# One column's rank-one term by the matmul engine in eight rounds, and a passage between two experts written in another order

## The chip, the core and the metric

The kernel runs on one core of one Trainium2 chip. Five engines work beside each other, each on a queue of its own: TensorE (PE, matmuls; its weight loads are listed as PEld), VectorE (DVE), ScalarE (ACT), GpSimd (POOL) and SyncE (SP), which sends the DMAs here. They wait for one another by semaphores. The metric is the device time of one execution in microseconds (us), the median over several runs.

## The reference

The kernel must compute this (numpy):

```
X = real(fft(fft(x, axis=1), axis=2))        # x: 2 x 3008 x 256
x = X.reshape(6016, 256)
h = x @ moe_w_in                              # 256 -> 2048
y = (h / (1 + exp(-h))) @ moe_w_out           # 2048 -> 256
h = y @ moe2_w_in                             # 256 -> 2048
g = max(h, 0) + moe2_alpha * min(h, 0)
out = g @ moe2_w_out                          # 2048 -> 256
```

Everything is fp32 outside the matmuls. To keep the accuracy of fp32, a factor of a matmul is split in two parts of type fp32r: `hi`, a rounded copy, and `lo`, the source less `hi`. A product is then three matmuls: hi by hi, lo by hi, hi by lo.

## The kernel before, in words

**Stages.** The transform is done as matrix products (64 by 47 points along the sequence, then 256 columns), with the symmetry of a real transform: tokens stand in pairs, and the 256 features are folded into sums and differences, 128 rows each. Of the 256 features, column 128 is left over by the folding. The 6016 tokens are six chunks of 502 pairs. A chunk's transformed features come out of PE as `ce` (even part), `co` (odd part) and `cn` (column 128, the same number on every row). ACT copies the first two into the hi parts of a tile `eo` (line 167, in `split`), DVE makes the low parts, and ACT copies `cn` into `n` (line 380).

**Expert 1** is 96 rounds, one for each chunk and each of 16 blocks of 128 hidden columns; `ORDER` lists them. The first eight rounds are blocks 0 to 7 of chunk 0. A round i does:
- `eo_mm`: the products `pe` (three matmuls, lines 562 to 564) and `po` (three) in PSUM;
- `silu_split`: DVE adds column 128's term, `t = n * w128 + pe` (line 570), where w128 is a column of 128 weights; then hp = t + po and t = t - po (lines 573, 574), the hidden values of the two tokens of a pair; ACT makes SiLU of each twice, as `gh` rounded and as fp32 (lines 577, 578);
- `low1` for the round before: the low parts `gl` of its two tiles (line 590), on POOL or DVE by `lo_pool`;
- `mm2` for the round two back (`LAG`): twelve matmuls with the weights `wo` into four accumulators (lines 612 to 616).

**Other work among the rounds.** The weights arrive as 64-bit numbers in pairs of 32-bit words (`raw_i`, `raw_o`, `w_raw`), and five steps turn a piece into fp32: ACT line 183, then four on DVE, the third on line 199. The pieces' splits, the transform of the other chunks (`z` is its middle stage, line 345 on ACT and 347 on DVE), and the preparation of expert 2's weights are divided among the rounds by `PLAN`: `put(a, b, steps)` spreads steps over rounds a to b - 1.

**Expert 2** goes by another scheme, in 96 items: seven products of sums and differences of blocks in place of eight, on `os` tiles (split sums of the first expert's output, made by `split_o1`, lines 650 to 660) and slabs `ws_*` of prepared weights (lines 514 to 523). Its items follow in written order: `outer` (two products into `ac`, which ACT copies to `e`, line 690), `inner` (three products), `seventh`, `fourth`, the PReLU by ACT and DVE, and `mm4`. Its output weights `wo` come from `v2o` by two sign steps on ACT for each half slab (line 542, scale by a column of `fc`) and a split (line 167 on ACT, 168 on POOL). The **passage** is where the last rounds of expert 1 (`mm2` of rounds 94 and 95) stand among the first items of expert 2.

**What sets the order.** The start, up to the first chunk's `eo` and n, and all of expert 2 are in written order (`tc.manual_schedule`). The rounds are ordered by a scheduler that plays the program on a time line; `leash` holds a round's extra steps behind given instructions of the rounds before. Within an engine's queue, nothing overtakes. SP's DMAs report on eight semaphores taken in turn (DMAHW0 to DMAHW7), and a DMA waits until the last one on its semaphore has landed.

## Time and profile before

| | us |
|---|---|
| median of 3 runs (lowest to highest) | 976.97 (976.53 to 977.37) |
| the profiled execution | 975.78 |
| its span on the core | 974.0 |
| mean granted TensorE clock | 0.996 of full speed |
| PE busy | 953.6 (98%) |
| DVE busy | 785.1 (81%) |
| ACT busy | 709.3 (73%) |
| POOL busy | 424.6 (44%) |

The span is what the profiler saw on the engines; the execution's own time has 1.8 us more around it. A row of a time line gives start, duration, engine, line, operation, output tile <- inputs, the shape, and in brackets the idle time of the engine ahead of it with what ended it. Several instructions of one form that follow each other stand as one row (x2). A tile's number is left out: `gl` stands for each of them. A wait put down to an instruction is the one that came last.

### The profile page before, as it was taken

The numbers are of one execution on the slowest core, as the hardware profiler recorded it, in microseconds if no ns is written. First come the engines' busy times: TensorE is split into PE (matmuls) and PEld (weight loads), VectorE is DVE, ScalarE is ACT, GpSimd is POOL, SyncE is SP. The second block draws the span as 40 slices with busy tenths as digits, with TensorE's granted clock in tenths as the row PEclk, the third lists the DMA queues.
The fourth block names the chain that finished last, engine by engine and source line by source line (L and its number), as shares of the span: only waits on it lengthen the run. The fifth ranks groups of instructions, "written<-read, shape, count | busy, mean of one in ns | idle before, by whom it ended". The sixth has DMA issues, their size and how long they took to land.

```text
span 974.0 us, 14393 instructions
## 1 busy us (share of the span) xinstructions
PE 953.6 (98%) x5186; PEld 821.7 (84%) x5186; DVE 785.1 (81%) x1319; ACT 709.3 (73%) x1410; POOL 424.6 (44%) x368
## 2 busy tenths in 40 slices
PE   8899999999999999999899999999999999999998
PEld 6578888788788888887789999999999999999997
DVE  5977888787696988997588787887878888787876
ACT  3557677575575757778788787888888888887875
POOL 2576889753257677799522131221222112131200
PEclk9989999999999999999999999999999999999999
DMA  8822000015101110100000000000000000000000
GB/s 269 284 78 87 1 1 22 22 28 174 44 1 60 44 61 27 44 1 1 1 1 22 1 22 23 1 22 1 23 22 1 22 1 22 22 1 22 1 23 21
DMA packets 16615, 37.06 MB, mean 38 GB/s; under 512 B 1824, under 2 KB 11296, under 8 KB 14880
## 3 DMA queue, kind: packets, MB, share of 16 engines
q1 hardware_dynamic: 16544, 36.15, 11.2%
q8 instruction: 40, 0.66, 0.3%
q14 instruction: 31, 0.25, 0.1%
HBM read 26.83 MB, written 9.31 MB: 37 GB/s over the span
## 4 chain that ended last, share of the span: by engine, by line
PE 87%; DVE 3%; POOL 3%; ACT 3%; issue 2%; DMA 0%; SPq 0%; POOLq 0%; DVEq 0%; ACTq 0%
PE a L772 27%; PE ac L674 20%; PE a L614 7%; PE a L616 7%; PE a L612 7%; PE b L674 3%; PE po L562 2%; PE po L564 2%; PE pe L562 2%; PE po L563 2%; PE pe L564 2%; PE pe L563 2%; POOL gl L590 2%; PE psb L327 1%; PE psa L283 1%
## 5 line engine op out<-in xcount | busy, mean ns | idle before, releaser
L772 PE MATMUL a<-gh,wo 128*128 128x502 f32 x768 | 268.2, 391 | 0.0
L772 PEld LDWEIGHTS a<-gh,wo 128*128 128x128 f32 x768 | 145.1, 189 | 23.3
L741 DVE SCALAR_TENSOR_TENSOR h<-h,fc,q 128x502 f32<-128x502 f32 x192 | 129.9, 676 | 38.0 <-ACT q L736 35.3
L590 POOL TENSOR_TENSOR gl<-t,gh 128x502 fp32r<-128x502 f32 x96 | 133.6, 1392 | 55.4 <-ACT t L578 44.5
L614 PE MATMUL a<-gl,wo 128*128 128x502 f32 x384 | 148.6, 396 | 4.0 <-POOL gl L590 2.9
L772 PE MATMUL a<-gl,wo 128*128 128x502 f32 x384 | 149.7, 391 | 0.0
L616 PE MATMUL a<-gh,wo 128*128 128x502 f32 x384 | 146.6, 392 | 0.0
L577 ACT ACTIVATE gh<-hp 128x502 fp32r<-128x502 f32 x96 | 59.8, 623 | 116.5 <-DVE hp L573 115.5
L752 DVE TENSOR_TENSOR gl<-h,gh 128x502 fp32r<-128x502 f32 x192 | 140.7, 733 | 0.1
L612 PE MATMUL a<-gh,wo 128*128 128x502 f32 x384 | 119.2, 393 | 2.4 <-ACT gh L577 2.3
L747 ACT ACTIVATE gh<-h 128x502 fp32r<-128x502 f32 x192 | 118.4, 617 | 2.1 <-DVE h L741 2.1
L590 POOL TENSOR_TENSOR gl<-hp,gh 128x502 fp32r<-128x502 f32 x65 | 90.1, 1386 | 68.1 <-ACT hp L578 66.5
L736 ACT ACTIVATE q<-h,fc 128x502 f32<-128x502 f32 x192 | 116.9, 609 | 2.8 <-DVE h L719 1.5
L650 POOL TENSOR_TENSOR xt<-o 128x252 f32<-128x252 f32 x24 | 16.7, 715 | 187.2 <-ACT q L736 149.8
L614 PEld LDWEIGHTS a<-gl,wo 128*128 128x128 f32 x384 | 73.1, 190 | 21.6 <-POOL gl L590 5.1
L570 DVE SCALAR_TENSOR_TENSOR t<-n,sm,pe 128x502 f32<-128x502 f32 x96 | 70.3, 732 | 25.5 <-PE pe L564 23.6
L612 PEld LDWEIGHTS a<-gh,wo 128*128 128x128 f32 x384 | 71.8, 189 | 18.7 <-ACT gh L577 4.0
L616 PEld LDWEIGHTS a<-gh,wo 128*128 128x128 f32 x384 | 73.1, 190 | 14.6
L772 PEld LDWEIGHTS a<-gl,wo 128*128 128x128 f32 x384 | 72.4, 189 | 7.6
L708 ACT ACTIVATE u<-ac 128x252 f32<-128x252 f32 x96 | 36.6, 381 | 54.2 <-PE ac L674 54.2
L573 DVE TENSOR_TENSOR hp<-t,po 128x502 f32<-128x502 f32 x96 | 64.5, 672 | 13.9 <-PE po L564 6.8
L660 POOL TENSOR_TENSOR os<-o,os 128x252 fp32r<-128x252 f32 x36 | 32.4, 912 | 92.4 <-ACT os L659 92.4
(191 smaller groups left out, 2294.0 us busy)
## 6 DMA issues: line engine op xcount, KB each, us to landing
out_t<-ot SPq DMA_DIRECT2D x24, 251.0 KB, 2.6
x<-in_xs SPq DMA_DIRECT2D x8, 512.0 KB, 5.4
raw_i<-in_wi SPq DMA_DIRECT2D x8, 512.0 KB, 6.2
raw_w<-in_wi SPq DMA_DIRECT2D x4, 1024.0 KB, 5.9
raw_w<-in_wo SPq DMA_DIRECT2D x4, 1024.0 KB, 4.8
raw_o<-in_wo SPq DMA_DIRECT2D x3, 1024.0 KB, 6.8
y<-ys SPq DMA_DIRECT2D x16, 144.0 KB, 3.4
x<-in_xs SPq DMA_DIRECT2D x2, 1024.0 KB, 4.7
```

Source lines behind the costliest of these rows:

```text
L570: nc.vector.scalar_tensor_tensor(t, E128[c], w128_sb[:, f : f + 1], pe, op0=ALU.mult, op1=ALU.add)
L573: nc.vector.tensor_tensor(hp, t, po, op=ALU.add)
L590: LAST["gl", i] = (nc.gpsimd if s or lo_pool(i + 1) else nc.vector).tensor_tensor(lo, h, hi.bitcast(F32), op=ALU.subtract)
L612: nc.tensor.matmul(ACC1[lb, s], hi, G[i, s][0], start=st, stop=False)
L614: nc.tensor.matmul(ACC1[lb, s], hi, G[i, s][1], start=False, stop=False)
L616: nc.tensor.matmul(ACC1[lb, s], lo, G[i, s][0], start=False, stop=sp)
L674: nc.tensor.matmul(to, w, x, start=start and q == 0, stop=q == 2, skip_group_check=True)
L736: nc.scalar.activation(h["q", i][:, to], source(n, part), AF.Abs, scale=coef(n, i, 1))
L741: nc.vector.scalar_tensor_tensor(h[f"h{i}"][:, to], source(n, part), coef(n, i, 0), h["q", i][:, to], op0=ALU.mult, op1=ALU.add)
L747: nc.scalar.activation(hi, H[n][f"h{i}"], AF.Copy)
L752: nc.vector.tensor_tensor(lo, H[n][f"h{i}"], G[n, i][0].bitcast(F32), op=ALU.subtract)
L772: nc.tensor.matmul(ACC2[lb], w[lb][j], x, start=st and first, stop=sp and last)
```

## The change

Two things are changed that have nothing to do with each other.

**Column 128 in the first eight rounds.** A tile `rank` of 96 rows is added. Its first 1024 columns (`RANK["w"]`) hold the weights of column 128 for hidden blocks 0 to 7: the hi part on row 0, the lo part on row 32, hi again on row 64, zeros elsewhere. The next 502 (`RANK["x"]`) hold n of chunk 0: its hi part on rows 0 to 63, its low part on rows 64 to 95. One matmul of 96 rows adds hi by hi, lo by hi and hi by lo to `pe`. ACT copies `pe` into t, and DVE's step on line 570 goes for these rounds. To fill the tile, the row of weights is loaded once more as 16 x 128 (`wrow`), turned into fp32 and split (`rank_split`); six DMAs on SP bring four rows at a time, as one row, into two cleared tiles `rank_s` (`rank_place`), and ACT copies those into `rank` (`rank_round`), ahead of the first chunk's `eo`.

**The passage.** The sign steps of expert 2's output weights get steps of their own in rounds 84 to 92 (`sg0` to `sg3`), where before they went with the splits; the splits of slabs 2 and 3 go to items 98 to 101, counted on from the 96 rounds. `split_o1(0)` is spread over rounds 89 to 93 in place of 91 to 94. `gl` of the last round is made by DVE for both tiles.

```diff
@@ -29,7 +29,8 @@
     "fa": (16, 17), "x": (24, 27, 32, 34), "a": (30, 33, 36, 38), "y0": (41, 42), "c3": (43, 48), "y1": (49, 50), "c4": (54, 61),
     "y2": (65, 66), "c5": (67, 77), "w2": (50, 88),
     "co": (60, 61), "ws0": (62, 80), "ws0b": (84, 92), "ws1": (80, 92), "ws1b": (93, 99),
-    "wo0": (86, 87), "wo1": (90, 91), "wo2": (97, 98), "wo3": (98, 100),
+    "sg0": (84, 86), "sg1": (87, 89), "sg2": (89, 91), "sg3": (91, 93),
+    "wo0": (86, 88), "wo1": (90, 92), "wo2": (98, 100), "wo3": (100, 102),
 }
 W2_AHEAD = 2
 HALF = 252
...
@@ -59,6 +60,7 @@
 A_VEC = lambda b, h, i: b and h and i == 0
 W2_ORDER = (0, 2, 4, 5, 1, 3, 6, 7)
 LO_POOL = 30
+RANK_F = 8
 K_PARTS = (0, 12, 24, 32)
 B_GROUPS = (0, 3, 6, 9, 12, 16)
 PAIRS = [(k0 + i, k0 + (k1 - k0) // 2 + i) for k0, k1 in zip(K_PARTS, K_PARTS[1:]) for i in range((k1 - k0) // 2)]
...
@@ -377,7 +382,12 @@
 
         def ny():
             E128[b * NCB + c] = n = ep.tile([128, CW], F32, tag="e128", name=f"n{b}_{c}", padded_shape=[128, 512])
-            LAST[b * NCB + c] = nc.scalar.activation(n, part("n", (ch, SG0, 0), (ch, SG0, 1)), AF.Copy)
+            ps = part("n", (ch, SG0, 0), (ch, SG0, 1))
+            if b * NCB + c == 0:
+                to = RANK["x"]
+                nc.scalar.activation(to, ps[:96], AF.Copy)
+                nc.vector.tensor_tensor(to[64:96], ps[64:96], to[64:96].bitcast(F32), op=ALU.subtract)
+            nc.scalar.activation(n, ps, AF.Copy)
 
         return [mixed] * (b > 0 or c == 2) + [ev, od, ny]
 
...
@@ -531,25 +541,56 @@
         return steps
 
     def prep_wo2(g):
-        def part(h):
-            if h == 0:
-                wo_tiles(2, g)
+        def signs(h):
             o = (g % 2) * 1024 + h * 512
             v = V2["o", g // 2][:, o : o + 512]
             for q in range(2):
                 f = 4 * g + 2 * h + q
                 w = v[:, 256 * q : 256 * q + 256]
                 nc.scalar.activation(w, w, AF.Copy, scale=fc[:, 2, f : f + 1])
+
+        def part(h):
+            if h == 0:
+                wo_tiles(2, g)
+            o = (g % 2) * 1024 + h * 512
+            v = V2["o", g // 2][:, o : o + 512]
             hi, lo = (WO[2, g, j].rearrange("p f e -> p (f e)")[:, h * 512 : h * 512 + 512] for j in range(2))
             split(hi, lo, v, nc.gpsimd)
 
-        return [lambda: part(0), lambda: part(1)]
+        return [lambda: signs(0), lambda: signs(1)], [lambda: part(0), lambda: part(1)]
 
 
     ACC1 = {}
     G = {}
     O1 = {}
     MORE = [False]
+
+    def rank_rows():
+
+        t = big([96, 2048], F32R, "rank")
+        RANK["w"], RANK["x"] = t[:, : 128 * RANK_F], t[:, 1024 : 1024 + CW]
+        u = xp.tile([128, 512], F32, tag="xs", name="rank_f")
+        RANK["f"] = [u[:NF, 128 * j : 128 * j + 128] for j in range(3)]
+        RANK["s"] = [xp.tile([128, 512], F32, tag="xs", name=f"rank_s{j}") for j in range(2)]
+        for u in RANK["s"]:
+            nc.gpsimd.memset(u[:96], 0.0)
+
+    def rank_split():
+        f, hi, lo = RANK["f"]
+        nc.scalar.activation(hi.bitcast(F32R), f, AF.Copy)
+        nc.vector.tensor_tensor(lo, f, hi, op=ALU.subtract)
+
+    def rank_place():
+        for n, u in enumerate(RANK["s"]):
+            for r, j in ((0, 0), (32, 1), (64, 0)):
+                nc.sync.dma_start(
+                    u[r : r + 1, :].rearrange("p (f m) -> p f m", m=128),
+                    RANK["f"][1 + j][4 * n : 4 * n + 4],
+                )
+
+    def rank_round():
+        for n, u in enumerate(RANK["s"]):
+            nc.scalar.activation(RANK["w"][:, 512 * n : 512 * n + 512], u[:96], AF.Copy)
 
     def eo_mm(i):
         c, f = ORDER[i]
...
@@ -561,13 +602,19 @@
             hi, lo = WI[1, g, j][:, sl], WI[1, g, j + 1][:, sl]
             nc.tensor.matmul(ps, hi, eo[:, j, :], start=True, stop=False)
             nc.tensor.matmul(ps, lo, eo[:, j, :], start=False, stop=False)
-            LAST["pe", i] = nc.tensor.matmul(ps, hi, eo[:, j + 1, :], start=False, stop=True)
+            whole = j or i >= RANK_F
+            LAST["pe", i] = nc.tensor.matmul(ps, hi, eo[:, j + 1, :], start=False, stop=bool(whole))
+        if i < RANK_F:
+            LAST["pe", i] = nc.tensor.matmul(pe, RANK["w"][:, 128 * f : 128 * f + 128], RANK["x"], start=False, stop=True)
         return pe, po
 
     def silu_split(i, pe, po):
         c, f = ORDER[i]
         t = work(F32, f"t{i}")
-        nc.vector.scalar_tensor_tensor(t, E128[c], w128_sb[:, f : f + 1], pe, op0=ALU.mult, op1=ALU.add)
+        if i < RANK_F:
+            nc.scalar.activation(t, pe, AF.Copy)
+        else:
+            nc.vector.scalar_tensor_tensor(t, E128[c], w128_sb[:, f : f + 1], pe, op0=ALU.mult, op1=ALU.add)
         low1(i - 1)
         hp = work(F32, f"hp{i}")
         nc.vector.tensor_tensor(hp, t, po, op=ALU.add)
...
@@ -584,10 +631,11 @@
     def low1(i):
         if i < 0:
             return
+        end = i == len(ORDER) - 1
         for s in range(2):
             hi, h = G[i, s]
             lo = work(F32R, f"gl{i}_{s}")
-            LAST["gl", i] = (nc.gpsimd if s or lo_pool(i + 1) else nc.vector).tensor_tensor(
+            LAST["gl", i] = (nc.gpsimd if not end and (s or lo_pool(i + 1)) else nc.vector).tensor_tensor(
                 lo, h, hi.bitcast(F32), op=ALU.subtract
             )
             G[i, s] = (hi, lo)
...
@@ -819,15 +868,19 @@
             load_o1(1)
             warm(cs[:, FA0 : FA0 + 128], cs[:, :256], WARM)
             (s0, p0), (s1, p1) = prep_o1(0)
+            rank_rows()
+            wrow_st = to_f32(lambda: RANK["f"][0], ("wrow", 0, 128), "wrow")[1]
             w128_st = to_f32(lambda: w128_sb, ("w128", 0, NF), "w128")[1]
             run(i00[:4])
             run(i01[:2])
-            run(w128_st[:1])
+            run(w128_st[:1] + wrow_st[:1])
             nc.scalar.activation(ch, cc, AF.Copy)
             run(i00[4:])
             for ab in zip(i01[2:], w128_st[1:]):
                 run(ab)
-            run(w128_st[4:])
+            run(w128_st[4:] + wrow_st[1:])
+            rank_split()
+            rank_place()
             nc.vector.tensor_tensor(cl, cc[:, : SG0 - CD0], ch.bitcast(F32)[:, : SG0 - CD0], op=ALU.subtract)
             for n, (st, pool) in enumerate(zip(after_i0, SUM0)):
                 (st if callable(st) else st[pool == "v"])()
...
@@ -838,6 +891,7 @@
             run(b01[:2])
             run(p0)
             run(s1[:EARLY_O0])
+            rank_round()
             run(stage_c(0, 0))
             rest(1)
             for h in range(2):
...
@@ -908,8 +962,10 @@
             put(*PLAN[f"ws{pg}"], steps[:8])
             put(*PLAN[f"ws{pg}b"], steps[8:])
         for g in range(4):
-            put(*PLAN[f"wo{g}"], prep_wo2(g))
-        put(n1 - 5, n1 - 1, split_o1(0))
+            first, then = prep_wo2(g)
+            put(*PLAN[f"sg{g}"], first)
+            put(*PLAN[f"wo{g}"], then)
+        put(n1 - 7, n1 - 2, split_o1(0))
 
         for i in range(n1):
             pe, po = eo_mm(i)
```

What is left out: the new input `wrow` (column 128's weights as 16 x 128), its raw tile and its load behind that of `w128`.

**How the order moves.** The rows that follow are the instructions as they stand in an engine's queue: line of the code, operation, output <- inputs, partitions x elements; x2 is two in a row.

SP at the start of the program, behind the load of the second piece of expert 1's weights (`raw_o`, `raw_i`). `ys` and `y` are stores and loads that carry the first chunk between two stages of the transform. In brackets stand the semaphores that a DMA waits on (here with the compiler's number). Before:

```order
L404 DMA raw_o_190<-in_wo 128x1024
L395 DMA raw_i_198<-in_wi 128x1024 x2
L395 DMA raw_o_201<-in_wo 128x2048 [waits DMAHW0_49]
L297 DMA ys_0_1_130<-ya_0_132 48x12x128 [waits DMAHW1_49]
L297 DMA ys_1_1_137<-ya_1_139 48x12x128 [waits DMAHW2_49]
```

The same place after the change:

```order
L414 DMA raw_o_192<-in_wo 128x1024
L405 DMA raw_i_200<-in_wi 128x1024 x2
L405 DMA raw_o_203<-in_wo 128x2048 [waits DMAHW1_49]
L586 DMA rank_s_228<-rank_f 1x4x128 [waits DMAHW2_49,Activation_49,Pool_49]
L586 DMA rank_s_228<-rank_f 1x4x128 [waits DMAHW3_49,DVE_49]
L586 DMA rank_s_228<-rank_f 1x4x128 [waits DMAHW4_49]
L586 DMA rank_s_229<-rank_f 1x4x128 [waits DMAHW5_49,Pool_49]
L586 DMA rank_s_229<-rank_f 1x4x128 [waits DMAHW6_49]
L586 DMA rank_s_229<-rank_f 1x4x128 [waits DMAHW7_49]
L302 DMA ys_0_1_132<-ya_0_134 48x12x128 [waits DMAHW0_49]
```

The six DMAs into `rank_s` stand between the last load of weights and the stores of `ys`; the last of them is the eighth DMA behind the first `raw_i` of this place and goes by the same semaphore.

ACT ahead of the first chunk's `eo`; `wo` and `cvo` are expert 1's output weights, z the middle stage of the transform. Before:

```order
L345 ACTIVATE z_1_271<-psb_1_3_283 128x63
L452 ACTIVATE wo_0_0_291<-cvo_0_251 128x512
L183 ACTIVATE cvo_1_295<-raw_o_190 128x512
L167 ACTIVATE eo_0_299<-ce_0_300 128x502
L167 ACTIVATE eo_0_299<-co_0_308 128x502
L380 ACTIVATE n_0_314<-cn_0_315 128x502
```

The same place after the change:

```order
L350 ACTIVATE z_1_292<-psb_1_3_304 128x63
L462 ACTIVATE wo_0_0_312<-cvo_0_272 128x512
L186 ACTIVATE cvo_1_316<-raw_o_192 128x512
L593 ACTIVATE rank<-rank_s_228 96x512
L593 ACTIVATE rank<-rank_s_229 96x512
L170 ACTIVATE eo_0_322<-ce_0_323 128x502
L170 ACTIVATE eo_0_322<-co_0_331 128x502
L388 ACTIVATE rank<-cn_0_338 96x502
L390 ACTIVATE n_0_337<-cn_0_338 128x502
```

Both copies of `rank_s` stand ahead of the first `eo`, and the copy of n into `rank` ahead of n.

POOL in the last rounds of expert 1, from the second `gl` of round 92 on: `v2w` and `ws_*` are expert 2's input weights, `os` the low parts of its first sums. Before:

```order
L590 TENSOR_TENSOR gl_1_4330<-t_4286,gh_1_4298 128x502
L523 TENSOR_TENSOR v2w_3354<-v2w_3354 128x512
L518 TENSOR_TENSOR ws_5l<-v2w_3354,ws_5h 128x512
L660 TENSOR_TENSOR os_1_4303<-o_0_741,os_0_4302 128x252 x2
L590 TENSOR_TENSOR gl_1_4373<-t_4326,gh_1_4338 128x502
L518 TENSOR_TENSOR ws_7l<-v2w_3354,ws_7h 128x512
L660 TENSOR_TENSOR os_1_4303<-xt_0_4261,os_0_4302 128x504
L660 TENSOR_TENSOR os_1_4303<-xt_1_4262,os_0_4302 128x504
L590 TENSOR_TENSOR gl_1_4416<-t_4369,gh_1_4381 128x502
L590 TENSOR_TENSOR gl_1_4432<-t_4412,gh_1_4424 128x502
```

The same place after the change:

```order
L638 TENSOR_TENSOR gl_1_4377<-t_4332,gh_1_4344 128x502
L533 TENSOR_TENSOR v2w_3387<-v2w_3387 128x512
L528 TENSOR_TENSOR ws_5l<-v2w_3387,ws_5h 128x512
L708 TENSOR_TENSOR os_1_4307<-xt_1_4216,os_0_4306 128x504
L533 TENSOR_TENSOR v2w_3387<-v2w_3387 128x512
L638 TENSOR_TENSOR gl_1_4418<-t_4373,gh_1_4385 128x502
L528 TENSOR_TENSOR ws_7l<-v2w_3387,ws_7h 128x512
L528 TENSOR_TENSOR ws_6l<-v2w_3387,ws_6h 128x512
L638 TENSOR_TENSOR gl_1_4457<-t_4414,gh_1_4426 128x502
```

Three steps of `os` leave the stretch from `gl` of round 92 to that of round 94, a difference of `v2w` and `ws_6l` come into it, and `gl` of round 95 is no longer POOL's.

## Rows read from the trace of the kernel before

**Rows 1.** Windows: us, busy us (count) of PE, PEld, DVE, ACT, POOL; clock, DMA share, GB/s.

```profile
30.00:65.00 35.00, 29.17 (x116) 21.20 (x115) 31.07 (x42) 19.13 (x37) 21.33 (x18) 0.90 0.51 170
65.00:450.00 385.00, 383.28 (x1724) 316.96 (x1723) 321.99 (x455) 257.01 (x467) 267.57 (x220) 1.00 0.13 42
450.00:490.00 40.00, 35.87 (x201) 30.05 (x200) 26.08 (x44) 33.24 (x71) 29.69 (x26) 1.00 0.01 1
...
48.80:52.00 3.20, 3.18 (x8) 2.58 (x9) 0.28 (x1) 3.17 (x7) 3.20 (x5) 0.50 0.66 246
```

**Rows 2.** Waits of PE: line <- what it waited for: us, times, longest us.

```profile
PE a L614 <- POOL gl L590: 2.9, 4, 1.7
...
PE ac L674 <- ACT e L690: 1.9, 2, 1.6
PE pe L562 <- DVE z L347: 1.9, 1, 1.9
```

**Rows 3.** The page's costliest groups: DVE's step for column 128.

```profile
L570 DVE SCALAR_TENSOR_TENSOR t<-n,sm,pe 128x502 f32<-128x502 f32 x96 | 70.3, 732 | 25.5 <-PE pe L564 23.6
```

**Rows 4.** Time line of PE at the passage.

```profile
460.42 0.39 PE L614 MATMUL a<-gl,wo 128*128 128x502 f32 x1
460.65 0.39 PE L616 MATMUL a<-gh,wo 128*128 128x502 f32 x1
461.38 0.39 PE L674 MATMUL ac<-os,ws_5h 128*128 128x252 f32 x1 [0.35 <-POOL os L660]
...
464.24 0.49 PE L614 MATMUL a<-gl,wo 128*128 128x502 f32 x1 [1.68 <-POOL gl L590]
...
472.33 0.49 PE L674 MATMUL ac<-os,ws_6h 128*128 128x252 f32 x2 [1.62 <-ACT e L690]
```

**Rows 5.** Time line of ACT round the first chunk's `eo`.

```profile
28.79 0.68 ACT L183 ACTIVATE cvo<-raw_o 128x512 f32<-128x512 f32 x1
30.18 0.59 ACT L167 ACTIVATE eo<-ce 128x502 fp32r<-128x502 f32 x1 [0.71 <-PE ce L357]
```

**Rows 6.** Time line of DVE, from the start to round 5.

```profile
21.55 0.17 DVE L199 SCALAR_TENSOR_TENSOR sm<-w_raw,sm 128x16 uint32<-128x16 uint32 x1
...
33.55 0.68 DVE L573 TENSOR_TENSOR hp<-t,po 128x502 f32<-128x502 f32 x1 [0.54 <-PE po L564]
...
48.40 0.68 DVE L574 TENSOR_TENSOR t<-t,po 128x502 f32<-128x502 f32 x1
...
57.42 0.44 DVE L347 TENSOR_TENSOR z<-psb,z 128x282 fp32r<-128x282 f32 x1
```

**Rows 7.** Time line of POOL in the last rounds of expert 1.

```profile
455.84 1.33 POOL L660 TENSOR_TENSOR os<-o,os 128x252 fp32r<-128x252 f32 x2
...
460.06 2.93 POOL L660 TENSOR_TENSOR os<-xt,os 128x504 fp32r<-128x504 f32 x2
...
466.63 1.30 POOL L518 TENSOR_TENSOR ws_6l<-v2w,ws_6h 128x512 fp32r<-128x512 f32 x1
```

**Rows 8.** Time line of SP's queue: the DMAs issued there.

```profile
22.32 0.91 SPq L395 DMA_DIRECT2D raw_i<-in_wi  x2
23.27 0.43 SPq L395 DMA_DIRECT2D raw_o<-in_wo  x1
24.06 1.47 SPq L297 DMA_DIRECT2D ys<-ya  x2
```

**Rows 9.** DMAs issued at 22.32, 23.27, 24.06: size, us to landing.

```profile
raw_i<-in_wi SPq DMA_DIRECT2D x1, 512.0 KB, 7.1
...
raw_o<-in_wo SPq DMA_DIRECT2D x1, 1024.0 KB, 10.0
...
ys<-ya SPq DMA_DIRECT2D x1, 288.0 KB, 10.1
```

**Rows 10.** The tile ys: DMAs to and from it.

```profile
DMA to landing us min/median/max: 2.0/3.4/10.5
```

**Rows 11.** Time line of ACT at the passage.

```profile
468.79 0.90 ACT L542 ACTIVATE v2o<-v2o,fc 128x256 f32<-128x256 f32 x2
```

More of the change, by code (lines that the diff above doesn't have):

```diff
@@ L128, in fft_moe_kernel @@
     w128: bass.AP,
+    wrow: bass.AP,
     wo1: bass.AP,
@@ L222, in fft_moe_kernel @@
     w128_raw = wp.tile([128, NF, 2], U32, name="w128_raw")
+    wrow_raw = wp.tile([NF, 128, 2], U32, name="wrow_raw")
+    RANK = {}
     fc = wp.tile([128, 3, NF], F32, name="fc")
@@ L388, in fft_moe_kernel @@
     WS = {}
-    RAW = {"w128": w128_raw}
+    RAW = {"w128": w128_raw, "wrow": wrow_raw}
     def load_raw(key, *srcs):
@@ L805, in fft_moe_kernel @@
                     nc.sync.dma_start(w128_raw.rearrange("p n t -> p (n t)"), w128.bitcast(U32))
+                    nc.sync.dma_start(wrow_raw.rearrange("p n t -> p (n t)"), wrow.bitcast(U32))
             nc.sync.dma_start(cs[:, R0:], cst[:, R0:CD0])
@@ L967, in fft_moe_kernel @@
                     seventh(n)
-_IN = ["xs", "cst", "wi1", "w128", "wo1", "wi2", "wo2", "alpha"]
+_IN = ["xs", "cst", "wi1", "w128", "wrow", "wo1", "wi2", "wo2", "alpha"]
 def kernel(x, moe_w_in, moe_w_out, moe2_w_in, moe2_w_out, moe2_alpha):
@@ L995 @@
         "w128": bits(moe_w_in[128].reshape(NF, 128).T),
+        "wrow": bits(moe_w_in[128].reshape(NF, 128)),
         "wo1": bits(rows(moe_w_out)),
```

## The prediction, made before the changed kernel ran

> **What bounds the kernel now.** I read the busy time by stretch first. From 65 to 450 us PE is busy 383.28 of 385.00 us, so what is saved on another engine there is worth nothing. From 30 to 65 us it is busy 29.17 of 35.00, at a granted clock of 0.90, and DVE 31.07 of 35.00; round the passage between the experts, 450 to 490, PE is busy 35.87 of 40.00 [rows 1]. The change touches just these two stretches. The 4.13 us missing at the passage are the most that it can give there. In the head 5.83 us are idle, and part of it runs at the lower of PE's two clocks, 1.2 instead of 2.4 GHz: from 48.8 to 52.0 the granted clock is 0.50, which costs 1.6 us [rows 1].
>
> The waits of PE over the whole execution then name the releasers: POOL's low parts `gl` 2.9 us, ACT's copy `e` 1.9 us, DVE's low part `z` 1.9 us in one wait [rows 2]. The wait on e and most of that on gl belong to the passage, that on z to the head. No wait on a DMA stands there.
>
> **The head, part by part.** Removed: eight DVE steps on line 570, at 732 ns [rows 3] 5.9 us, five of them (3.7 us) before 58 us, in DVE's fullest stretch. Added on PE: eight matmuls. Successive matmuls of 502 columns start 0.23 us apart [rows 4]; no row has one of 96 rows by 502 columns, so a price between 0 and 0.39 us, and I take 0.23, because the columns are the same: 1.8 us. Added on ACT: eight copies of pe, of a form whose nearest row is 0.59 us (128x502 out of PSUM) [rows 5], 4.7 us in all, and each is on the way from pe to hp, as the DVE step was; then three copies of 96 rows, between 0.59 and 0.68 [rows 5]: I take 0.62. Added on DVE: five steps on 16 rows at 0.17 [rows 6], 0.85 us, with the handover to ACT and back about 1.3 us, and a low part of 32 rows that I put at 0.67, by the 0.68 of 128 rows [rows 6]. The two clears on POOL and the small load of the row are costed at nothing: they run under the loads of x and raw_i, when POOL has little to do; without that cover they cost about one POOL step, 1.30 us [rows 7].
>
> What decides is a wait that the change adds. Six small DMAs put the hi and lo parts of column 128 on rows 0, 32 and 64 of `rank_s`. On SP they stand behind the load of raw_o, and ACT copies `rank_s` in two instructions that stand ahead of its first copy of `eo`. Each DMA also waits on one of eight DMA semaphores, taken in turn, so that it goes out only once the eighth DMA before it has landed. For the last of the six this is the first half of raw_i, issued at 22.32 [rows 8] and landed 7.1 us later [rows 9]: 29.4. The loads land in the order of their issue: raw_o of 23.27 [rows 8] after 10.0 us, at 33.3, and a store sent at 24.06, right behind it [rows 8], after 10.1 us, at 34.2 [rows 9]. I let the six small ones land behind raw_o: 33.4. ACT is free at 29.47 (28.79 + 0.68), and its first `eo` copy started at 30.18 [rows 5]. Now: 33.4 + 2 x 0.62 = 34.7, 4.5 us late. All of ACT's queue stands behind it; DVE's low parts of `eo` and PE's first pe wait for that copy. (DVE's 1.3 us alone would delay z, and with it this copy, to about 31.5; the 33.4 covers it.) The bound from below: if the queue held nothing, 29.4 + 2.0 for the fastest landing of a transfer of ys in the trace [rows 10], + 1.24 = 32.6, 2.5 us late.
>
> The Trainium skill, DMA: Bandwidth & Descriptors, section Queues, rings and completion order, says that each DMA engine takes one queue's descriptors in ring order, but that a DMA on few engines may be reported complete ahead of an earlier one on all sixteen. By its section on why a semaphore goes up by 16, a copy of four rows runs on four engines. The ring order speaks for the 33.4; the completion rule for something earlier, and with 32.6 in place of 34.7 the head would lose 2.1 us less. No run here shows a small transfer behind a load.
>
> From `eo` on I follow the instructions of the first rounds with before's durations. Rank product: ACT copies x (0.6), DVE makes its low part (0.67), PE adds a product, ACT copies t (0.6), where before one DVE step stood: +0.8, so the first hp starts at 33.55 [rows 6] + 5.3 = 38.9. Rounds 1 to 3 lose three DVE steps (2.2 us), but hp of a round now waits for an ACT copy that stands behind three silus of the round before (about 2.5 us in line); DVE's two last conversion passes also come before round 2's hp. The two cancel but for some tenths: round 3's t, at 48.40 before [rows 6], comes 6.0 us later. The order then puts z's low part, at 57.42 before [rows 6], ahead of one conversion pass: pe of round 5 (counted from 0), which waited for it, is 4.8 us late. From there PE has a backlog; three more rank products (0.7 us), less 0.3 us of a small wait that goes. The head: **+5.2 us**, with +2 (fast landing, some relief) and +7 (another stretch at the lower clock, as that of 1.6 us before) as its ends.
>
> **The passage.** The e copy of the second product waited 1.62 us [rows 4], because ACT had four sign steps (0.90 for two) and two wo copies ahead of it, from 468.79 on [rows 11]. These are gone from there; e follows PE's product at once. With the second, shorter wait on e, 1.9 us go [rows 2]. The 0.35 us on os [rows 4] goes too, as the split ends earlier. But the 1.68 us [rows 4] on `gl` of round 94 are POOL's queue, and that gets no shorter. Between `gl` of rounds 92 and 94 two steps of os 128x252 (1.33 together) and one of two os 128x504 (2.93 together) leave, 2.80 us; a v2w difference and ws_6l, both at ws_6l's 1.30 us [rows 7], come in, 2.60. The sign steps now stand in the ACT queue of rounds 84 to 92, two pairs of them (1.8 us) ahead of the silus that POOL reads for rounds 91 and 92; I let 0.6 us of it reach POOL. So `gl` of round 94 ends 0.4 us later, and since PE waits there anyway, the 0.35 of os is swallowed: +0.4 - 1.9 = **-1.5 us**. `gl` of round 95 on DVE is hidden by DVE's wait for the first b; uncovered it would cost up to two steps of 0.67. The ends: -3.5 (POOL in time, so that its 1.68 and the os wait go as well) and -0.5 (ACT reaching POOL with all its 1.8 us).
>
> **Sum.** +5.2 - 1.5 = +3.7 us. The profiled execution took 975.78 us (974.0 of span and 1.8 around it), so 979.5; the median of the runs shown is 1.2 us above it, 976.97, and so 980.7. I say 980.5.
>
> **The rivals.** *Rows in time, relief decides.* If the six DMAs land before 29.5, when ACT is ready, the first `eo` copy is late by DVE's 1.3 us only, and the first hp by 0.8 more. With 3.7 - 0.7 = 3.0 us less on DVE before 58 us, and DVE as the path, pe of round 5 comes 0.9 us early; the three later products cost 0.7, and the 1.6 us at the lower clock may go too. The head gives 0.2 to 1.8 us, and with -1.5 to -3.5 at the passage the time is 971.7 to 975.3, 973.5 in the middle. For it speaks how full DVE is [rows 1]; against it the landings [rows 9], and that the last DMA is held until 29.4. It decides from a landing below 30.
>
> *Rows land at about 31.5, between.* Then 2.1 us less are lost in the head, or the relief is worth two of the three steps instead of cancelling: +2.5 to +3.1, and with the passage at -1.5 to -2.5 some 977 to 978.5. The completion rule that the Trainium skill states would lead here.
>
> *POOL takes over the passage.* If `gl` of rounds 91 to 94 come later by ACT's whole 1.8 us, the passage gives 0.5, and with a head of +7 the time is 983.5 to 984.
>
> *The passage doesn't get shorter at all:* its wait moves from ACT to POOL. This is inside my forecast for the POOL part; alone it moves the time by 1 us.
>
> **How the numbers follow.** My forecast has 0.50 (978.5 to 983), the rows between 0.21, relief 0.19, the POOL case 0.10. A measurement of this kernel can tell about 0.2%, or 1.95 us: faster is below 975.0, slower above 978.9. Faster: nearly all of relief and a little of the one between, 0.19. Slower: the POOL case, and 0.45 of the forecast, 0.55. Same: the rest, 0.26. The range 973.5 to 984 leaves out the lower half of relief, and little above. The forecast's own is 978.5 to 983.
>
> **What would show it.** Right: in the profile after, ACT idle before line 593 until about 33.4, released by a DMA of `rank_s`; the first `eo` copy near 34.7; pe of round 5 some 5 us later than 57.9; PE's wait on e at the passage gone, and one on POOL's `gl` of 1.5 us or more still there. Wrong: line 593 starting by 31, or the first 60 us no longer than before; no wait on `gl` at the passage; or new PE waits in rounds 84 to 92, which I put at none.

## The result and the profile after

The changed kernel took 985.1 us (median of 5 runs, 981.25 to 988.05) against 976.97 for the kernel before (975.65 to 977.37): a ratio of 1.0081, interval 1.0063 to 1.0099. It is slower by 8.1 us, where 3.7 were forecast. Its profiled execution has a span of 982.4 us, 8.4 more than before.

The busy time by stretch [rows 1], and then three stretches in which the clock was low (columns as there):

```profile
30.00:65.00 35.00, 29.37 (x112) 21.33 (x113) 25.20 (x39) 21.34 (x42) 19.17 (x15) 0.90 0.41 130
65.00:450.00 385.00, 380.71 (x1713) 313.96 (x1713) 320.86 (x449) 258.34 (x472) 265.77 (x219) 1.00 0.14 44
450.00:490.00 40.00, 36.71 (x181) 31.20 (x180) 27.62 (x43) 28.84 (x60) 25.27 (x20) 0.91 0.01 1
...
30.30:33.70 3.40, 3.40 (x9) 2.79 (x9) 2.03 (x6) 1.11 (x3) 1.28 (x1) 0.50 0.64 200
54.20:57.60 3.40, 3.40 (x12) 2.79 (x11) 0.51 (x1) 3.23 (x7) 3.40 (x5) 0.50 0.00 0
470.60:477.40 6.80, 5.72 (x18) 5.04 (x19) 1.31 (x3) 1.10 (x2) 1.02 (x1) 0.50 0.00 0
```

DVE has indeed 5.9 us less to do between 30 and 65 (25.20 for 31.07), and PE hardly more than before (29.37 for 29.17). In the long middle, which the prediction left alone, PE is idle 4.3 us where it was idle 1.7. At the passage it is idle less (3.3 for 4.1 us), but the granted clock there is 0.91, where it was 1.00.

The waits of PE [rows 2], with PE's wait on z in the kernel before under them, and then the head: SP's queue [rows 8], the landing of its raw_o [rows 9] and ACT's queue [rows 5]:

```profile
PE a L662 <- POOL gl L638: 5.8, 6, 2.9
PE ce L362 <- DVE z L352: 2.6, 1, 2.6
PE po L603 <- DVE t L621: 1.9, 2, 1.2
```

```profile
28.67 0.70 PE L357 MATMUL ce<-z,ch 128*128 128x502 f32 x2 [0.79 <-DVE z L347]
```

```profile
23.03 0.45 SPq L405 DMA_DIRECT2D raw_o<-in_wo  x1
23.58 5.70 SPq L586 DMA_DIRECT2D rank_s<-rank_f  x6
30.00 2.83 SPq L302 DMA_DIRECT2D ys<-ya  x2
```

```profile
raw_o<-in_wo SPq DMA_DIRECT2D x1, 1024.0 KB, 9.4
```

```profile
33.13 1.16 ACT L593 ACTIVATE rank<-rank_s 96x512 fp32r<-96x512 f32 x2 [2.29 <-DMA rank_s<-rank_f]
34.19 0.57 ACT L170 ACTIVATE eo<-ce 128x502 fp32r<-128x502 f32 x1
```

The wait on the `rank_s` DMAs is there as forecast: ACT stands 2.29 us, the copy starts at 33.13 (forecast 33.4), the first eo copy at 34.19 (34.7), and pe of round 5 at 62.22, 4.3 us later (some 5). SP was done with sending the six at 29.28 (29.4). The wait on e at the passage is gone. One wait has grown: PE stands 2.6 us for z ahead of `ce`, where it stood 0.8. One is new: PE waits twice on DVE's t, far behind the head. For that one, DVE, POOL and PE between 149 and 162 us:

```profile
151.20 4.92 DVE L190 TENSOR_SCALAR cvo<-cvo 128x512 f32<-128x512 f32 x1 [1.27 <-ACT cvo L186]
156.05 0.66 DVE L621 TENSOR_TENSOR t<-t,po 128x502 f32<-128x502 f32 x1
```

```profile
150.85 1.29 POOL L447 TENSOR_TENSOR wi<-cvi,wi 128x512 fp32r<-128x512 f32 x1
152.11 1.26 POOL L638 TENSOR_TENSOR gl<-hp,gh 128x502 fp32r<-128x502 f32 x1
153.33 1.26 POOL L638 TENSOR_TENSOR gl<-t,gh 128x502 fp32r<-128x502 f32 x1
154.56 1.27 POOL L638 TENSOR_TENSOR gl<-hp,gh 128x502 fp32r<-128x502 f32 x1
```

```profile
156.76 0.49 PE L603 MATMUL po<-eo,wi 128*128 128x502 f32 x1 [0.73 <-DVE t L621]
161.40 0.49 PE L603 MATMUL po<-eo,wi 128*128 128x502 f32 x1 [1.20 <-DVE t L621]
```

A DVE step that takes 0.42 us at other places (line 190, 128x512) took 4.92. It starts 0.35 us into a POOL step, POOL goes through four steps without a gap, and the DVE step ends (156.12) when POOL's queue runs dry (155.83). t, and with it the PSUM buffer that `po` needs, are late. In the kernel before, the same step (line 187 there) also starts inside a POOL step, 0.39 us after its start, and POOL goes on without a gap there, too, but the DVE step gets in after the first POOL step:

```profile
147.56 1.22 DVE L187 TENSOR_SCALAR cvo<-cvo 128x512 f32<-128x512 f32 x1 [1.32 <-ACT cvo L183]
```

```profile
147.18 1.33 POOL L437 TENSOR_TENSOR wi<-cvi,wi 128x512 fp32r<-128x512 f32 x1
148.43 1.49 POOL L590 TENSOR_TENSOR gl<-hp,gh 128x502 fp32r<-128x502 f32 x1
```

At the passage, PE's wait on `gl` of round 94 has grown from 1.68 [rows 4] to 2.91 us, and the clock falls in it:

```profile
471.68 0.79 PE L662 MATMUL a<-gl,wo 128*128 128x502 f32 x1 [2.91 <-POOL gl L638]
```

To place the loss, the matmuls of two traces were matched in order by their tiles. The table gives by how many us they start later than in the profile of before (median of those within 1.5 us of the time at the column's head), and the timed ratio to before with its interval.

```
kernel          100us  140us  250us  400us  900us   ratio (interval)
before again     -0.5   -0.5   -0.4   -0.4   +1.2
after            +3.3   +3.7   +6.4   +6.1   +8.7   1.0081 (1.0063-1.0099)
after again      +5.2   +5.6  +12.4  +12.1  +13.6   1.0078 (1.0049-1.0106)
rank_only        +5.3   +5.7   +5.6   +5.3   +6.8   1.0083 (1.0066-1.0100)
rank_no_dma      +2.2   +2.6   +5.3   +5.0   +5.1   1.0043 (1.0028-1.0059)
rank_late        +2.3   +2.8   +5.4   +5.2   +6.5   1.0041 (1.0027-1.0055)
rank_late_gap    +1.7   +2.2   +2.9   +2.8   +3.1   1.0037 (1.0024-1.0050)
rank_no_conv     -1.3   -0.7   +1.9   +1.7   +1.8   1.0001 (0.9989-1.0013)
passage_only     -1.2   -1.2   -1.1   -1.1   +1.4   1.0017 (1.0008-1.0027)
signs_alone      -1.2   -1.2   -1.2   -1.2   -2.1   0.9961 (0.9948-0.9973)
passage_gl94     -0.8   -0.8   -0.8   -0.8   -3.4   0.9956 (0.9943-0.9969)
signs_gl         -0.7   -0.6   -0.6   -0.6   -3.1   0.9977 (0.9964-0.9990)
```

So in the profile of after: 3.3 us by the head, 2.7 between 140 and 250, and 2.6 from the passage on.

### The profile page after: what moved, and what is told of

Same layout as the page of the kernel before. It is cut to its first block, busy times and chain, and to the rows that moved or that the text cites. A ratio compares the mean times of both kernels' runs of the same rounds, so it can differ in the third digit from the quotient of the medians.

```text
span 982.4 us, 14432 instructions
## 1 busy us (share of the span) xinstructions
PE 958.9 (98%) x5194; PEld 825.6 (84%) x5194; DVE 788.8 (80%) x1318; ACT 714.5 (73%) x1423; POOL 424.9 (43%) x369
## 4 chain that ended last, share of the span: by engine, by line
PE 48%; DVE 2%; ACT 1%; POOL 0%; issue 0%
PE a L820 25%; PE ac L722 19%; PE b L722 3%; DVE h L789 1%; DVE gl L800 1%; ACT q L784 0%; ACT gh L795 0%; PE a L664 0%; PE a L662 0%; DVE h L752 0%; POOL ws_7l L528 0%; POOL ws_6l L528 0%; DVE h L767 0%; PE a L660 0%; POOL gl L638 0%
## 5 line engine op out<-in xcount | busy, mean ns | idle before, releaser
L789 DVE SCALAR_TENSOR_TENSOR h<-h,fc,q 128x502 f32<-128x502 f32 x192 | 131.5, 685 | 33.4 <-ACT q L784 30.6
L638 POOL TENSOR_TENSOR gl<-t,gh 128x502 fp32r<-128x502 f32 x95 | 131.3, 1382 | 57.6 <-ACT t L625 47.4
L800 DVE TENSOR_TENSOR gl<-h,gh 128x502 fp32r<-128x502 f32 x192 | 144.6, 753 | 0.1
L617 DVE SCALAR_TENSOR_TENSOR t<-n,sm,pe 128x502 f32<-128x502 f32 x88 | 64.4, 732 | 25.1 <-PE pe L606 24.7
```

The costliest lines, as they stand in the source:

```text
L617: nc.vector.scalar_tensor_tensor(t, E128[c], w128_sb[:, f : f + 1], pe, op0=ALU.mult, op1=ALU.add)
L638: LAST["gl", i] = (nc.gpsimd if not end and (s or lo_pool(i + 1)) else nc.vector).tensor_tensor(lo, h, hi.bitcast(F32), op=ALU.subtract)
L789: nc.vector.scalar_tensor_tensor(h[f"h{i}"][:, to], source(n, part), coef(n, i, 0), h["q", i][:, to], op0=ALU.mult, op1=ALU.add)
L800: nc.vector.tensor_tensor(lo, H[n][f"h{i}"], G[n, i][0].bitcast(F32), op=ALU.subtract)
```

## The experiments

**The changed kernel once more** (no edit).

> The changed kernel once more, for a second profile of it. Its first profile is 8.4 us longer than the profile of before: 3.3 us by 100 us, 2.9 us between 145 and 162 us, where one DVE step (line 190) took 4.92 us instead of 0.42 while POOL ran without a gap, and 2.1 us at the passage, where the granted clock was 0.51 for 6.8 us behind a 2.91 us wait of PE on POOL's gl. Theory C (the 2.9 us is a collision that comes and goes): the long DVE step is not there in this profile, or stands elsewhere, and the span differs by about 3 us. Rival S (the order fixes it): the same step takes over 3 us again. The wait on gl and the lower clock at the passage come from the order by both: 2.5 to 3.2 us and one stretch near 470.

983.45 us, 980.24 to 989.38. The profile is that of the slowest execution (989.38). Two long DVE steps this time:

```profile
153.12 4.90 DVE L190 TENSOR_SCALAR cvo<-cvo 128x512 f32<-128x512 f32 x1 [1.32 <-ACT cvo L186]
179.71 5.55 DVE L638 TENSOR_TENSOR gl<-hp,gh 128x502 fp32r<-128x502 f32 x1
```

The first is the same step, with the same 2.8 us behind it (rival S). The second is another one, in a stretch where POOL again ran five steps without a gap; with the low clock behind it, it cost 4.0 us. It came in one profile of the two (theory C). PE's wait on `gl` at the passage is there again with 2.93 us, and the low clock behind it with 3.4. The head costs 5.2 us here, not 3.3: the low clock lasted 6.8 us from 32.0, where it was 3.4 from 30.3.

**The kernel before once more** (no edit).

> The kernel before, for a second profile: which of its waits and long DVE steps are the same in two executions. Theory C: single DVE steps of over 3 us may stand in it too, at other places; waits on gl 1.7 and on e 1.6 at the passage are there again. Time 975.5 to 977.5.

976.98 us. No DVE step over 2.2 us, and the two waits at the passage as in the first profile (1.69 on gl, 1.64 on e). But the clock fell for 3.4 us at the passage (PE busy in all of it, so 1.7 us lost), which the first profile does not have: that loss comes and goes in the kernel before, too.

**The rank product alone**: the `PLAN` entries, `split_o1(0)` and `gl` of round 95 as before.

> Column 128 by PE in eight rounds as in the change, the passage as before. If the head and the passage add up: the head costs 3.3 us, plus up to 2.9 where the long DVE step stands, and the passage is the one of before: 980 to 983, a ratio of 1.0034 to 1.0065. Rival (the head alone is harmless and all of it comes from the passage): 976 to 978. In the profile: rows land at about 33.1, first eo copy at 34.2, PE at 100 us 3.3 us late; waits on gl near 1.7 and on e near 1.6 at the passage, clock full there.

984.31 us, above the 980 to 983 expected. By the times, all of the loss of the whole change is there. In its profile the head costs 5.3 us, and the step on line 190 (189 here) took only

```profile
153.24 1.23 DVE L189 TENSOR_SCALAR cvo<-cvo 128x512 f32<-128x512 f32 x1 [1.29 <-ACT cvo L185]
```

so nothing is lost between 140 and 250. That execution, at 982.57 us, is the fastest of the four timed (the others took up to 985.35); whether those had the long step is not shown.

**The passage alone**: rank product out, the rest of the diff kept.

> The passage as in the change, the head as before. Theory P (POOL's gl of round 94 is late by its own queue, and the wait lets the clock fall): PE waits 2.5 to 3.2 us on gl, the e wait is gone, the clock falls for 3.4 to 6.8 us, and the time is 977 to 980. Rival Q (that wait comes from the head's delay and is not there without it): the passage gives its 1.5 us and the time is 975.0 to 976.

978.47 us, +1.7 by the ratio. PE's wait on gl of round 94 is there with the head of before (theory P, not Q), and the clock was low from 462.9 to 469.7:

```profile
464.52 0.79 PE L620 MATMUL a<-gl,wo 128*128 128x502 f32 x1 [2.91 <-POOL gl L596]
```

```profile
462.90:469.70 6.80, 5.17 (x17) 4.57 (x18) 0.84 (x2) 1.05 (x2) 1.57 (x2) 0.50 0.00 0
```

PE was busy 5.17 us of these at half its speed, so some 2.6 us are lost, as much as the passage costs from 400 to 900 us (2.5). The two parts measured alone add up to more (8.1 and 1.7 us by the ratios) than the whole change (7.9 and 7.6 by its two ratios); within the intervals of the ratios these agree, so the runs don't tell whether the parts add up.

**Without the six DMAs**, the passage as before, as in all experiments on the rank product (column 128's term is left out of the first eight rounds, `rank_s` being zero).

```diff
-            rank_place()
```

> Column 128 by PE as in the change, the passage as before, but without the six small DMAs: rank_s stays at zero, so the term of column 128 is left out of the first eight rounds. Theory W (the wait for the landing is what the head loses): ACT's first copy of rank_s starts near 30.8 instead of 33.1, the first eo copy near 31.5, and PE at 100 us is 2.5 to 4 us earlier than in the run with the DMAs (there 5.3 us later than before): a time of 979 to 981, and under 978.5 if the low clock of the head goes too. Rival A (the ACT copies in line and the added matmuls are the cost): PE at 100 us is still 4 us or more late, time 982 to 984. The long DVE step between 150 and 162 us (4.9 us in both executions of the whole change, not in the one of this part alone) stays open: if it is chance it may be there or not, worth 2.8 us.

981.3 us. PE is 3.1 us less late at 100 us than with the DMAs: theory W. Some of that is the clock, which was low for 3.4 us in this head and for 10.2 us in that of rank_only; against the first profile of the whole change (3.3 us late, low for 3.4) it is 1.1. But the times part as well, with intervals that do not overlap. 2.2 us of the head are still there, because the first eo copy is still 2.6 us late, where 31.5 was expected for it:

```profile
30.91 1.13 ACT L592 ACTIVATE rank<-rank_s 96x512 fp32r<-96x512 f32 x2
32.74 0.59 ACT L169 ACTIVATE eo<-ce 128x502 fp32r<-128x502 f32 x1 [0.70 <-PE ce L361]
```

It waits for PE now. The step on line 189 took 4.94 us again.

**The product from round 2 on**, its ACT copies behind eo and n.

```diff
+RANK_FROM = 2
...
-            rank_round()
             run(stage_c(0, 0))
+            rank_round()
...
-        if i < RANK_F:
+        if RANK_FROM <= i < RANK_F:
```

> The product with column 128 in rounds 2 to 7 alone, ACT's two copies of rank_s behind the copies of eo and n, n copied ahead of its copy into rank; passage as before. Theory W: the wait for the landing lies where ACT has nothing else to do (until about 34), the first eo copy starts near 30.2 to 31.5, PE at 100 us is 0 to 1.5 us later than before, time 976 to 979. Rival A: 980 to 983.

981.91 us, in the range of rival A and above theory W's 976 to 979. The copies of `rank_s` no longer stand ahead of eo, and still PE waits for z and eo comes at 32.87:

```profile
30.40 1.18 PE L362 MATMUL ce<-z,ch 128*128 128x502 f32 x2 [2.59 <-DVE z L352]
```

```profile
32.87 0.59 ACT L170 ACTIVATE eo<-ce 128x502 fp32r<-128x502 f32 x1 [1.74 <-PE ce L362]
```

Two matmuls of `ce` take 1.18 us, where 0.70 is their time at full clock (below): it was low from 28.7 to 35.5, while PE stood for z.

**The same without the conversion of the row** (`rank_f` cleared by POOL instead, so column 128's term is left out of rounds 2 to 7).

```diff
+        nc.gpsimd.memset(u[:NF, :384], 0.0)
...
-            wrow_st = to_f32(lambda: RANK["f"][0], ("wrow", 0, 128), "wrow")[1]
...
-            run(w128_st[:1] + wrow_st[:1])
+            run(w128_st[:1])
...
-            run(w128_st[4:] + wrow_st[1:])
-            rank_split()
+            run(w128_st[4:])
```

> As the run with the product late (rounds 2 to 7, copies of rank_s behind eo and n), but without the five DVE steps and two ACT steps that turn the row of weights into fp32 and split it: rank_f is cleared by POOL, so column 128's term is left out of these rounds. In the late run PE still waited 2.6 us on z ahead of ce, its first eo copy started at 32.87, and PE was 2.3 us late at 100 us. Theory V (the small DVE steps push the conversion of raw_o and with it z, ce and eo back, and the idle PE then runs at the lower clock from 28.7): the wait on z is under 1.2 us, the first eo copy starts before 31.2, PE at 100 us is within 0.8 us of before, and the time is 2 to 3 us less than the late run's 981.9: 979 to 980, or 976 to 978 if the long DVE step near 150 is not there. Rival A (the ACT copies and the matmuls in the first rounds cost it): PE at 100 us still 2 us late or more.

977.09 us, a ratio of 1.0001. Theory V holds: the wait on z is 0.82 us as in the kernel before (0.8), eo comes at 30.27 (30.18 before), the clock does not fall in the whole head, and PE is 1.3 us early at 100 us. That is not the gain of the product: five profiles with the head of before are 0.5 to 1.2 us early there, too, and in the first profile of before the clock was low for 6.8 us of the head, in two stretches.

```profile
28.76 0.70 PE L362 MATMUL ce<-z,ch 128*128 128x502 f32 x2 [0.82 <-DVE z L352]
```

```profile
30.27 0.59 ACT L170 ACTIVATE eo<-ce 128x502 fp32r<-128x502 f32 x1 [0.75 <-PE ce L362]
```

```profile
146.76 4.92 DVE L190 TENSOR_SCALAR cvo<-cvo 128x512 f32<-128x512 f32 x1 [1.27 <-ACT cvo L186]
```

The long step is there all the same, and costs 2.6 us.

**A gap in POOL's queue**: rank_late, with one `gl` of rounds 23 and 24 on DVE.

```diff
-        return i < LO_POOL or 52 <= i < 88
+        return i < LO_POOL and i not in (24, 25) or 52 <= i < 88
```

> As the run with the product late, but gl of one tile of rounds 23 and 24 is made by DVE, not POOL, so that POOL's queue has two steps less between 150 and 158 us. Theory L (the DVE step on line 190 stands still for 4.9 us because POOL goes from one step to the next without a gap, and PE loses 2.8 us by it): that step takes under 2.5 us, PE loses under 1 us between 140 and 165 us, and the time is 978.5 to 980 against 981.9. Rival E (the step waits for something else, or DVE pays the two steps itself): a loss of 2 us or more there, time 981 to 983.

```profile
150.38 0.93 DVE L190 TENSOR_SCALAR cvo<-cvo 128x512 f32<-128x512 f32 x1
```

```profile
149.28 1.75 POOL L447 TENSOR_TENSOR wi<-cvi,wi 128x512 fp32r<-128x512 f32 x1
150.99 1.46 POOL L637 TENSOR_TENSOR gl<-t,gh 128x502 fp32r<-128x502 f32 x1
153.35 1.78 POOL L637 TENSOR_TENSOR gl<-t,gh 128x502 fp32r<-128x502 f32 x1 [0.90 <-ACT t L625]
```

The step takes 0.93 us, and from 140 to 250 us 0.7 us are lost in place of 2.6: the loss goes with the long step. But theory L is not shown by it. The DVE step ended at 151.31, just after the first POOL step, as in the kernel before; POOL's gap came only at 152.45. And rank_only, without a gap, had no long step either, so one profile can't tell a cure from chance. The times (980.2 us, and intervals that overlap with rank_late's) don't resolve it.

**The passage with gl of round 94 on DVE too.**

```diff
-        end = i == len(ORDER) - 1
+        end = i >= len(ORDER) - 2
```

> The passage alone, with gl of round 94 made by DVE too (one instruction moved from POOL to DVE). Theory P: PE's 2.9 us wait on gl goes down to under 1 us, the clock is not lower behind it, and the time is 974.0 to 976.0, a ratio of 0.997 to 0.999. Rival D (DVE is as full there, and its own queue takes the wait's place): a wait on DVE of 1.5 us or more, time 976.5 to 978.5.

973.05 us, a ratio of 0.9956 (0.9943 to 0.9969): faster than both kernels, and than the 974 to 976 expected. PE's longest wait on gl is now

```profile
460.72 0.50 PE L620 MATMUL a<-gl,wo 128*128 128x502 f32 x1 [0.91 <-POOL gl L596]
```

and the clock stays up at the passage. One instruction moved from POOL to DVE turns +2.5 from 400 to 900 us into -2.6.

**The sign steps alone.**

```diff
-    "wo0": (86, 88), "wo1": (90, 92), "wo2": (98, 100), "wo3": (100, 102),
+    "wo0": (86, 87), "wo1": (90, 91), "wo2": (97, 98), "wo3": (98, 100),
...
-        put(n1 - 7, n1 - 2, split_o1(0))
+        put(n1 - 5, n1 - 1, split_o1(0))
...
-        end = i == len(ORDER) - 1
+        end = False
```

> Of the passage only the sign steps are moved into rounds 84 to 92; split_o1, the splits of wo and gl of round 95 as before. If the sign steps ahead of e were the cause of its 1.6 us wait, that wait is under 0.5 us, and if POOL's delay at the passage comes from the moved os and ws steps, the wait on gl stays at 1.7: time 974.5 to 976.0. Rival (the sign steps in ACT's queue delay the silus that POOL reads): the wait on gl grows to 2.5 or more and the time is 976.5 to 978.5.

973.34 us, 0.9961, below the 974.5 to 976.0 expected. The wait on e is gone, and the one on gl is what it was:

```profile
462.67 0.63 PE L620 MATMUL a<-gl,wo 128*128 128x502 f32 x1 [1.69 <-POOL gl L596]
```

So the sign steps in ACT's queue do not delay POOL. What is left for the delay is the other part of the passage, POOL's own order; which of its moved steps does it, no run separates. The clock was low for 3.4 us behind this wait, too.

**The sign steps, and gl of rounds 94 and 95 on DVE** (`end = i >= len(ORDER) - 2` in the kernel above).

> The sign steps moved into rounds 84 to 92 and gl of rounds 94 and 95 on DVE, split_o1 and the splits of wo as before. Theory P: the wait on gl (1.7 us with the signs alone) goes too and the time is 971 to 973. Rival D (DVE's queue takes its place): 973 to 975.

974.86 us, 0.9977, above the 971 to 973 of theory P and in rival D's range, but not by D's reason, DVE's queue. The wait on gl is replaced by one on `os`, which stood hidden behind it:

```profile
461.83 0.38 PE L680 MATMUL ac<-os,ws_5h 128*128 128x252 f32 x1 [1.48 <-POOL os L666]
```

It is no better than either of the two before it.

## Why the prediction was wrong

The direction was right and the size was not: +3.7 us forecast, +8.1 and +6.7 measured in two sets of runs. The first median, 985.1, is above the range of 973.5 to 984; the second, 983.45, is inside it, but above the forecast's own 978.5 to 983. Two steps failed: the term for the passage, and the long middle, which the sum leaves out. The head came out near its term, in part by luck.

*"+0.4 - 1.9 = -1.5 us"* for the passage. The 1.9 us on e did go. But `gl` of round 94 came 1.2 us later against PE, not 0.4 (PE took it up at 471.68 for 464.24 [rows 4], 7.4 us later, where its other matmuls just ahead are 6.2 late). The prediction priced the two steps that come into POOL's queue at 1.30 us each; they took 1.76 and 1.69:

```profile
464.10 1.76 POOL L533 TENSOR_TENSOR v2w<-v2w 128x512 f32<-128x512 f32 x1
...
468.73 1.69 POOL L528 TENSOR_TENSOR ws_6l<-v2w,ws_6h 128x512 fp32r<-128x512 f32 x1
```

Four of the last seven POOL steps ahead of this `gl` took 1.7 us, where such steps take 1.3 at other places, and they are all in line. From the start of `gl` of round 92 to the end of that of round 94, POOL needed 0.9 us more than before, where the prediction had 0.2 less. That first `gl` started 0.3 us late against PE, where the prediction had let 0.6 us of ACT's sign steps through. And the sum has no term for the clock at the passage. Of the waits on gl and on e, 1.68 and 1.62 us, one of 2.91 was left, and PE ran at half clock for 3.4 to 6.8 us behind it in all three profiles that have this passage, and in neither where `gl` of round 94 is DVE's. PE's idle time at the passage fell by 0.8 us; the low clock gave back 2.9 (5.72 us busy at half speed). By the run of the passage alone the term is +1.7, not -1.5. Since the clock fell there in three of seven profiles with the passage of before, and in that of signs_alone, too, the wait makes it likelier and is not its only cause. The rival that POOL takes over the passage had the right place, with 1.0 us.

*"The change touches just these two stretches"*, with what is between 65 and 450 us put at nothing. That was argued from gains only, by how busy PE is there; the sum has no loss for it. (The sign *"new PE waits in rounds 84 to 92, which I put at none"* held: the new waits are at 156 and 161 us.) With the rank product, a DVE step that got in behind one POOL step in the kernel before waits for four. It is there in five of the six profiles of kernels with the rank product ahead of the experiment with the gap, each time 4.90 to 4.94 us, and in none of the six without it; it costs 2.6 to 2.8 us. Why the rank product brings it is open. In all twelve the step starts 0.35 to 0.39 us into a POOL step, so its place against POOL's steps does not decide. Nor does the delay: in rank_no_conv PE is 0.7 us early at 140 us, as in the kernels without the product, and the step is long. The Trainium skill, SBUF — State Buffer, section SBUF: two separate sides, has the rule: DVE (in a mode with two ports, or with two inputs in SBUF against a GpSimd step that reads there) and GpSimd share a pair of ports, whoever starts first holds it for the whole instruction, and the other stands still. The trace agrees where the step took 1.20 to 1.23 us, in the other seven of the twelve profiles: it ended 0.3 us behind the POOL step that ran when it started. Where it took 4.9 us, the trace agrees that DVE stood while POOL worked; but by the rule it would have been one POOL step, and it was four.

*The head, +5.2 us*, came out at 3.3, 5.2 and 5.3 us in three profiles. The clock that is low from about 30 us on is part of each of these, and the sum has such a stretch only in its upper end of +7; that is the luck. The wait on the DMAs was read rightly: raw_o was issued at 23.03 and took 9.4 us, so it landed at 32.4, and the copy that waited for the small ones started at 33.13. That agrees with the ring order that the Trainium skill states (DMA: Bandwidth & Descriptors, Queues, rings and completion order), and an earlier completion did not show. (The stores of ys, behind the six in SP's queue, went out at 30.00 for 24.06; but the loads of y behind these at 33.78 for 34.34, no later, so that this is not the loss.) But the sum had one part too small. "The 33.4 covers it" was said of DVE's 1.3 us. In the changed kernel it does, but by itself this part costs more than the 31.5 that the prediction gives for it: z's low part came 1.44 us late, PE stood 2.6 us for it, the clock fell, and in rank_late the first eo copy was at 32.87 without a wait on a DMA.

```profile
28.08 1.65 DVE L347 TENSOR_TENSOR z<-psb,z 128x283 fp32r<-128x283 f32 x6
```

```profile
29.52 1.65 DVE L352 TENSOR_TENSOR z<-psb,z 128x283 fp32r<-128x283 f32 x6
```

(The first row is the kernel before, the second the changed one.) At 100 us the conversion of the row, with the clock behind it, costs 3.6 us (rank_late less rank_no_conv), and the DMAs 3.1 or less on top of it (rank_only less rank_no_dma, with the clock in it, as said above). What is left, -1.3 us, is hardly more than the 0.5 to 1.2 that profiles with the head of before are early, so that the relief which the rival "relief decides" sees in the product (its head costs 0.2 to 1.8 us) is neither shown nor excluded. What the rows do show is that the preparation of the row keeps the product from coming in time, and not the landing alone. Between one execution and the next the head differs by 2 us, with the length of the low clock (3.4 to 10.2 us).

## What to carry to other kernels

Before a step is cut from a full engine, look at what its replacement needs ahead of the first use: here tiny preparations on the same engine, put at 1.3 us, cost 3.6 with the clock behind them, and no run shows a gain from the eight long steps cut. A wait that grows is not priced by its own length alone: where PE stands for 2 to 3 us in one piece, look at the granted clock behind it. Where a change doesn't touch a stretch at all, DVE steps that run beside a gapless POOL queue can still lose several us, so take more than one profile and compare the longest instance of each form.

## What the runs showed that was not expected

- A DVE step of 0.42 us can stand for 4.9 us, one of 0.67 for 5.55, beside four or five POOL steps without a gap. The first of these got in behind one POOL step, with 1.20 to 1.23 us, in seven other profiles, with the same start inside a POOL step.
- The clock was low for 3.4, 6.8 or 10.2 us at a time, at the same places of a program in some executions and not in others, behind stretches in which PE had stood. The spread of the changed kernel (981.25 to 988.05) fits such losses and the long DVE steps, but only the two profiled executions show them.
- Moving one 1.3 us instruction from POOL to DVE was worth 5 us in the profile and 6 by the ratios (passage_only against passage_gl94).
